# Sigmoid attention and a swish MLP on one core: the table of steps made anew

## The chip, the core and the metric

The kernel runs on one core of one Trainium2 chip. The metric is the device time of one execution in microseconds, the median of several runs. The engines are TensorE (PE: matmuls; PEld: its weight loads), VectorE (DVE), ScalarE (ACT), GpSimd (POOL) and SyncE (SP). Each works through its own queue in order, and they meet at semaphores.

## The reference, cut to what matters

```python
batch, n_heads, seq, head_dim = (8, 12, 448, 64)
n_tokens, d_model, d_ff = (3584, 768, 2048)

# attention, per batch and head
scores = scale * np.matmul(q, k.transpose(0, 1, 3, 2)) - np.log(S)
attn = 1.0 / (1.0 + np.exp(-scores))
attn_out = np.matmul(attn, v)
# heads side by side: one row of 768 for each of 8 * 448 tokens
x = attn_out.transpose(0, 2, 1, 3).reshape(B * S, H * D)
# the MLP
h = x @ w_in
g = h * (1.0 / (1.0 + np.exp(-beta * h)))
out = g @ w_out
```

Inputs and output are float32; the kernel computes in fp16 with sums in PSUM in float32.

## The kernel before, in words

The work is cut into 24 groups of four heads (three groups for each of the 8 batches), and the MLP into batches of 448 tokens and, for the second product, pairs of 128-token tiles. The first batch's MLP is a plain product (`dense1`, `dense2`). From the second batch on both products of the MLP go by a Strassen-Winograd scheme: seven half-size products P1 to P7 instead of eight, for which weights, tokens and hidden values have to be added up first, in fp16.

Nothing in the code decides the order of the work but a table written into it. `OPENING + STEPS` is a list of 842 short names; `follow` walks it and calls one function for each name, and each engine's queue gets its instructions in that order. The names that matter here:

- `V g.jt` (`visit`): the scores of group g for one block of 128 keys: 8 matmuls on TensorE (L239), then two sigmoids on ScalarE (L251). The last block (jt 3) has 64 keys, and there two groups are done together: 16 matmuls, which need the transposes of both.
- `R g.r` (`transpose`): VectorE transposes the queries (r 0, L217) or keys (r 1, L225 and L229) of group g. `Q g` loads them from GpSimd's queue (L133) into one of three buffers named in `RAW_HOMES`.
- `K b` (`load_v`): v of batch b, six DMAs from GpSimd's queue (L153 four times, L160 twice), into one of two buffers. `E b` (`double_v_last`): VectorE copies its last rows (L167). `A g` (`attend`): attention times v for group g, 16 matmuls (L321) and two casts to fp16 on VectorE (L335).
- `X b.i` (`token_sum`): fp16 sums of tokens on VectorE, xs or xT. `S`, `T` (`weight_sum`): fp16 sums of the weights, w_S and w_T, once for all batches. `H t.i` (`hidden_sum`): fp16 sums of hidden values, "sum".
- `I b.d.i` (`wino1`): product Pi of the MLP's first half for batch b and block d: six matmuls of 224 columns (L192), then a sum or sigmoid. P1 opens PSUM bank x and P2 fills it further, P7 opens z and P4 fills it further, after VectorE has added up what P7 left. A product that fills a bank further has to wait for that.
- `G b.d`, `B b.d.j` (`weigh_right`, `weigh_below`): two or one sigmoids on ScalarE, and a product into gt on GpSimd (L520 for G, L530 for B).
- `U t.i.part` (`wino2`): half of product Pi of the second half for tiles t and t + 1: four matmuls of 384 columns (L192). Finished tiles are stored from SP's queue.
- `D`, `f`, `O`: the plain products of the first batch; `l`, `k`, `w`, `o`: loads of q, k and weights in the opening; `h`, `y`, `z`, `r`: visits, attention and transposes of half a group in the opening.

All sums, fp16 or not, go through one helper, `add`, so they share the line L406; the tile names tell them apart: "osb" has an input in PSUM, "w_T", "w_S", "xs", "xT" and "sum" are fp16 in SBUF throughout. Dense matmuls have one helper too, L192. It splits each of them into two of 64 columns when the next attention or score step in the table is an `A` or `y`:

```python
tiled["cols"] = D if then in ("A", "y") else P
```

Output buffers, and the buffers for q and k, are taken from seven homes, in the order of `OUT_HOMES` and `RAW_HOMES`.

Of the kernel before, what the change touches and what calls it, by code (L numbers as in the profile page):

```python
# [13 lines left out]
def kernel(  # L14
# [390 lines left out]
    def add(out, in0, in1, op=ALU.add):  # L405
# [275 lines left out]
    def follow(steps):  # L681
# [30 lines left out]
        B2.2.0 R12.0 V11.2 I2.3.4 U6.1.0 H6.2 U6.1.1 B2.3.0 B2.3.1 V12.2 I3.0.1 U6.2.0 H6.0
        H6.1 U6.2.1 A11 G2.3 X3.0 V12.1 X3.2 U6.6.0 U6.5.0 X3.1 U6.6.1 U6.5.1 V12.3 I3.0.2
        Q15 H6.3 K5 I3.0.6 U6.3.0 I3.0.5 U6.3.1 X3.3 I3.0.7 V12.0 Q18 I3.0.3 G3.0 H8.0
        U6.7.0 I3.0.4 H8.1 B3.0.0 U6.7.1 A12 V13.1 U8.1.0 H8.2 R15.1 U6.4.0 U6.4.1 U8.5.0
        U8.6.0 R14.1 E5 R15.0 Q16 U8.1.1 V13.2 U8.6.1 H8.3 U8.5.1 I3.1.1 U8.2.0 V13.0 U8.3.0
        U8.2.1 I3.1.6 U8.3.1 U8.7.0 B3.0.1 I3.1.5 U8.7.1 I3.1.7 I3.1.2 R14.0 I3.1.3 U8.4.0
        I3.1.4 U8.4.1 V14.2 I3.2.1 G3.1 R16.0 I3.2.6 A13 V14.0 Q17 B3.1.0 I3.2.2 I3.2.5
        B3.1.1 I3.2.7 I3.3.1 I3.2.3 V14.1 I3.2.4 I3.3.6 B3.2.0 I3.3.5 G3.2 U10.1.0 R16.1
        I3.3.2 I3.3.7 B3.2.1 I3.3.3 V14.3 I3.3.4 B3.3.1 I4.0.1 H10.2 B3.3.0 X4.0 U10.1.1 A14  # L720
        H10.0 X4.1 V15.2 G3.3 U10.2.0 U10.2.1 H10.1 I4.0.2 U10.5.0 V16.1 U10.6.0 U10.6.1
        I4.0.6 U10.5.1 U10.7.0 H10.3 I4.0.5 H12.0 X4.3 X4.2 V15.1 U10.3.0 R17.1 U10.7.1
        U10.3.1 V15.0 H12.2 I4.0.3 U10.4.0 U10.4.1 R17.0 R18.0 U12.1.0 Q19 H12.1 K6 A15
# [140 lines left out]
```

## Time and profile before

| | |
|---|---|
| median of 3 runs | 369.17 us (369.03 to 369.20) |
| the profiled execution | 369.55 us |
| its span in the profile | 367.7 us |
| granted TensorE clock | 0.998 |
| TensorE busy | 360.5 us, 98% |
| VectorE, ScalarE, GpSimd busy | 277.7, 248.0, 157.3 us |

Times in the profile run from the start of the span. A row of the timeline has the start and the duration in us, engine, line, operation, what it writes and reads, shapes, and how many instructions it merges; in brackets stand the idle time of the engine before it and what ended that. Matmuls are pipelined, and their ends are modelled, so the distance from start to start is the safer measure of them.

### The profile page before, as it was taken

The numbers are of one execution on the slowest core, as the hardware profiler recorded it, in microseconds if no ns is written. First come the engines' busy times: TensorE is split into PE (matmuls) and PEld (weight loads), VectorE is DVE, ScalarE is ACT, GpSimd is POOL, SyncE is SP. The second block draws the span as 40 slices with busy tenths as digits, with TensorE's granted clock in tenths as the row PEclk, the third lists the DMA queues.
The fourth block names the chain that finished last, engine by engine and source line by source line (L and its number), as shares of the span: only waits on it lengthen the run. The fifth ranks groups of instructions, "written<-read, shape, count | busy, mean of one in ns | idle before, by whom it ended". The sixth has DMA issues, their size and how long they took to land.

```text
span 367.7 us, 9364 instructions
## 1 busy us (share of the span) xinstructions
PE 360.5 (98%) x3795; PEld 238.6 (65%) x3795; DVE 277.7 (76%) x524; ACT 248.0 (67%) x410; POOL 157.3 (43%) x192
## 2 busy tenths in 40 slices
PE   8999999999999999999999999999999999999996
PEld 3577754466456875657865777657856587788564
DVE  5346768989886697867869767797898477889574
ACT  5988976886766797654984778777976568436210
POOL 7734513117514376611762433922541227228400
PEclk9999999999999999999999999999999999999999
DMA  8999999909179111953309040686001230010225
GB/s 169 188 200 198 200 204 204 228 9 123 25 158 145 42 34 18 180 117 85 55 7 194 16 92 3 120 100 138 3 0 45 45 87 2 0 34 11 46 70 187
DMA packets 42699, 34.77 MB, mean 95 GB/s; under 512 B 21904, under 2 KB 39200, under 8 KB 42656
## 3 DMA queue, kind: packets, MB, share of 16 engines
q0 software_dynamic: 36688, 22.47, 44.3%
q1 hardware_dynamic: 5968, 11.71, 12.1%
q8 instruction: 29, 0.48, 0.5%
q14 instruction: 14, 0.11, 0.1%
HBM read 45.62 MB, written 11.01 MB: 154 GB/s over the span
## 4 chain that ended last, share of the span: by engine, by line
PE 85%; DMA 5%; DVE 4%; POOL 4%; issue 1%; ACT 1%; DVEq 0%; ACTq 0%; POOLq 0%
PE m_ps L192 67%; PE sco L239 10%; PE av_ps L321 8%; DMA raw<-in_q_dram 3%; POOL gt L530 2%; DMA raw<-in_k_dram 2%; DVE osb L406 2%; DVE sum L406 1%; POOL w_in L174 1%; ACT sg L459 1%; POOL raw L133 1%; DVE w_T L406 1%; DVE xs L406 0%; DVE xT L335 0%; DVE qT L217 0%
## 5 line engine op out<-in xcount | busy, mean ns | idle before, releaser
L251 ACT ACTIVATE attnT<-sco 128x896 f16<-128x896 f32 (+1 forms) x163 | 139.3, 908 | 59.1 <-PE sco L239 58.5
L406 DVE TENSOR_TENSOR osb<-m_ps,osb 128x448 f32<-128x448 f32 (+2 forms) x197 | 115.3, 595 | 47.8 <-PE m_ps L192 40.8
L192 PEld LDWEIGHTS <-w_in 128*128 128x128 f16 (+1 forms) x1014 | 81.1, 101 | 20.3 <-issue 12.9
L530 POOL TENSOR_TENSOR gt<-osb,sg 128x448 f16<-128x448 f32 x52 | 60.6, 1180 | 67.5 <-ACT sg L459 65.6
L192 PE MATMUL m_ps<-xT,w_in 128*128 128x224 f16 (+3 forms) x804 | 84.2, 267 | 0.0
L459 ACT ACTIVATE sg<-osb,beta_sb 128x448 f32<-128x448 f32 (+1 forms) x104 | 54.7, 578 | 9.3 <-DVE osb L406 9.1
L192 PEld LDWEIGHTS <-sum 128*128 128x128 f16 (+1 forms) x456 | 39.8, 100 | 27.3 <-issue 5.2
L520 POOL TENSOR_TENSOR gt<-osb,sg 128x448 f16<-128x448 f32 x26 | 30.4, 1172 | 58.3 <-ACT sg L459 55.5
L239 PE MATMUL sco<-qT,kT 32*128 32x448 f16 (+3 forms) x864 | 51.5, 340 | 1.4 <-DVE kT L229 0.5
L192 PEld LDWEIGHTS <-gt 128*128 128x128 f16 (+1 forms) x484 | 37.4, 103 | 23.7 <-issue 6.1
L192 PE MATMUL m_ps<-w_out,gt 128*128 128x384 f16 (+2 forms) x340 | 52.7, 323 | 0.0
L192 PEld LDWEIGHTS <-w_S 128*128 128x128 f16 (+1 forms) x516 | 44.1, 100 | 7.8 <-issue 4.9
L192 PE MATMUL m_ps<-w_out,sum 128*128 128x384 f16 (+1 forms) x232 | 41.1, 327 | 0.0
L192 PE MATMUL m_ps<-w_T,sum 128*128 128x384 f16 (+1 forms) x224 | 40.8, 327 | 0.0
L321 PE MATMUL av_ps<-attnT,v 128*64 128x448 f16 (+3 forms) x400 | 38.0, 343 | 0.0
L192 PE MATMUL m_ps<-xs,w_S 128*128 128x224 f16 (+1 forms) x342 | 36.5, 259 | 0.4 <-DVE xs L406 0.4
L335 DVE CAST xT<-av_ps 128x448 f16<-128x448 f32 (+1 forms) x54 | 28.2, 564 | 8.3 <-PE av_ps L321 8.2
L133 POOL DMA_DIRECT2D raw<-in_q_dram x26 | 15.0, 579 | 42.0 <-DVE qT L217 16.4
L321 PEld LDWEIGHTS <-v 128*64 128x64 f16 (+1 forms) x432 | 20.8, 108 | 17.2 <-issue 8.2
L459 ACT ACTIVATE osb<-m_ps,beta_sb 128x224 f32<-128x224 f32 x52 | 20.3, 451 | 12.5 <-PE m_ps L192 11.5
L239 PEld LDWEIGHTS <-kT 32*128 32x128 f16 (+1 forms) x864 | 13.3, 96 | 23.8 <-issue 19.9
L363 DVE TENSOR_TENSOR gt<-m_ps,sg 128x224 f16<-128x224 f32 (+1 forms) x40 | 16.3, 432 | 11.9 <-ACT sg L360 11.8
(53 smaller groups left out, 310.0 us busy)
## 6 DMA issues: line engine op xcount, KB each, us to landing
out_dram<-osb SPq DMA_DIRECT2D x100, 96.0 KB, 1.9
raw<-in_k_dram POOLq DMA_DIRECT2D x23, 224.0 KB, 5.4
raw<-in_q_dram POOLq DMA_DIRECT2D x21, 224.0 KB, 3.8
v<-in_v_dram POOLq DMA_DIRECT2D x32, 144.0 KB, 6.5
w_in<-in_moe_w_in_dram POOLq DMA_DIRECT2D x8, 384.0 KB, 10.7
w_out<-in_moe_w_out_dram POOLq DMA_DIRECT2D x4, 768.0 KB, 13.5
v<-in_v_dram POOLq DMA_DIRECT2D x16, 48.0 KB, 6.1
out_dram<-osb SPq DMA_DIRECT2D x4, 192.0 KB, 2.1
```

The costliest lines, as they stand in the source:

```text
L133: nc.gpsimd.dma_start(out=raws[g][:, r, c0:c1].rearrange("p c d -> p (c d)"), in_=(q, k)[r][b, HQ * t : HQ * (t + 1)].rearrange("h (p c) d ...
L174: nc.gpsimd.dma_start(out=w_in16[:, :, c * n : (c + 1) * n], in_=moe_w_in[:, c * n : (c + 1) * n].rearrange("(c p) f -> p c f", p=P),)
L192: nc.tensor.matmul(to[c : c + step], hidden[:, c : c + step], weights, **({} if step == P else {"tile_position": (0, c)}), **flags,)
L239: nc.tensor.matmul(sco[base : base + nk, hh, u0 : u0 + n], kT[g][lo : lo + BLK, jt * P : jt * P + nk, e], qT[g][lo : lo + BLK, c0 : c0 + n ...
L251: nc.scalar.activation(out=at[:, :, 0:n], in_=sco[:, :, 0:n], func=AF.Sigmoid, bias=NEG_LOG_S, scale=MSCALE,)
L321: nc.tensor.matmul(av[hh * D : (hh + 1) * D, 0:n], vs[b][base : base + nk, 2 * (s % NPAIR) + hh, jt], at[base : base + nk, hh, 0:n], start ...
L335: nc.vector.tensor_copy(out=xTs[b][:, s % NPAIR, c0 : c0 + n], in_=av[:, 0:n])
L363: nc.vector.tensor_tensor(out=gt[:, dc, off : off + n], in0=m1[:, 0:n], in1=sg[:, 0:n], op=ALU.mult)
L406: nc.vector.tensor_tensor(out=out, in0=in0, in1=in1, op=op)
L459: nc.scalar.activation(out=out, in_=in_, func=AF.Sigmoid, bias=0.0, scale=beta_sb[:, dc : dc + 1])
L520: nc.gpsimd.tensor_tensor(out=gt[:, 2 * d : 2 * d + 2, off : off + QH], in0=ob[:, 0], in1=sg, op=ALU.mult)
L530: nc.gpsimd.tensor_tensor(out=gt[:, dc, off : off + S].rearrange("p (h n) -> p h n", h=2), in0=oa[:, :, j], in1=sg, op=ALU.mult,)
```

## The change

The same set of steps is put in another order: `OPENING`, `STEPS`, `RAW_HOMES` and `OUT_HOMES` are made anew, and no other line differs. No function changes, and no step is added or dropped. The change says of itself that VectorE's fp16 sums and GpSimd's products are kept apart in it by when each is ready.

As nearly every line of the table differs, here are the stretches that the prediction speaks of, old and new, with the steps around them.

```diff
-    RAW_HOMES = "012012012012201202121021"
+    RAW_HOMES = "012012012012012020120120"
...
 # opening
-    h0.1.0 y1.0 Q3 z1.0 h0.1.1 r1.1 y2.0 w6 Q4 z2.0 h1.1.0 w7 f0 f3 p0 f1 f4 r2.1 h1.1.1
-    f2 K1 f5 o0.0 y0.1 Q5 z0.1 h2.1.0 f6 f7 o1.0 f9 f8 o0.1 h2.1.1
+    y1.0 z1.0 w5 h0.1.1 r1.1 Q3 y2.0 w6 z2.0 Q4 p0 w7 h1.1.0 f3 f1 f0 f4 K1 r2.1 h1.1.1
+    f2 f5 o0.0 y0.1 z0.1 h2.1.0 f6 Q5 f7 f8 f9 o1.0 o0.1 h2.1.1
...
 # from A6 to A9, old
-    O1.1.7 E2 D1.10 R8.0 D1.2 V6.3 T1.0 D1.11 R10.0 D1.0 X1.3 A6 V7.1 D1.9 T1.1 D1.1
-    I1.3.1 X1.2 I1.2.1 V7.0 R8.1 I1.3.6 I1.3.5 I1.3.2 I1.2.2 I1.3.7 I1.3.3 Q9 V7.2
-    I1.3.4 I1.2.6 K3 I1.2.5 T4.1 U2.1.0 I1.2.7 B1.3.0 I1.2.3 B1.3.1 V8.0 I1.2.4 B1.2.0
-    H2.2 U2.1.1 A7 B1.2.1 V8.1 U2.2.0 H2.0 H2.1 X2.0 T4.0 R9.0 U2.2.1 U2.7.0 G1.3 R9.1
-    V8.2 U2.5.0 U2.6.0 U2.6.1 U2.5.1 H2.3 G1.2 V8.3 U2.7.1 A8 V9.1 U2.4.0 R10.1 Q13 H4.0
-    U4.1.0 U2.3.0 R11.1 V9.2 H4.1 U2.3.1 U4.1.1 U4.6.0 Q12 X2.1 H4.2 V9.0 U2.4.1 U4.6.1
-    X2.2 R11.0 E3 I2.0.1 R13.1 U4.2.0 X2.3 A9 V10.3 U4.2.1 I2.0.2 I2.0.6 U4.5.0 H4.3
...
-    S3.0 U4.5.1 Q14 I2.0.5 V10.0 K4 U4.7.0 U4.3.0 U4.3.1 V10.1 I2.0.3 G2.0 I2.0.7 U4.7.1
 # from A6 to A9, new
+    D1.1 V6.0 T2.1 D1.8 D1.0 V6.3 Q10 O0.1.7 S4.0 I1.3.1 T2.0 K4 A6 R9.1 R10.0 V7.1
+    D1.10 D1.11 X1.2 V7.0 I1.3.6 I1.3.2 I1.3.5 I1.2.1 X1.3 I1.3.7 I1.3.3 V7.2 I1.3.4
+    B1.3.1 I1.2.6 I1.2.5 B1.3.0 I1.2.7 R8.0 I1.2.2 I1.2.3 I1.2.4 R9.0 H2.2 S3.0 G1.3
+    V8.0 U2.1.0 U2.1.1 Q11 B1.2.0 B1.2.1 A7 H2.0 V8.1 U2.7.0 U2.2.0 H2.1 R10.1 G1.2
+    U2.2.1 T4.0 X2.0 V8.2 U2.5.0 U2.6.0 U2.6.1 U2.5.1 H2.3 V8.3 H4.0 U2.7.1 A8 V9.1 H4.1
+    U2.3.0 Q12 U2.3.1 U4.5.0 X2.1 V9.2 T4.1 U4.1.0 U4.1.1 H4.2 U4.6.0 K3 U4.6.1 U4.2.0
+    R11.1 V9.0 U2.4.0 R12.0 H4.3 X2.3 R11.0 U2.4.1 R12.1 E3 Q16 U4.2.1 U4.7.0 U4.5.1 A9
...
 # behind the last visit, old
-    B6.3.0 V23.1 U20.2.0 H20.0 H20.1 G6.3 U20.2.1 A23 U20.7.0 X7.0 I7.0.1 X7.1 I7.1.1
-    U20.6.0 X7.2 U20.6.1 H20.3 I7.0.6 U20.5.0 X7.3 I7.0.5 I7.0.2 I7.1.6 I7.0.7 U20.5.1
 # behind the last visit, new
+    I6.1.2 I6.1.3 I6.3.1 I6.1.4 V23.1 U18.7.0 B6.1.0 I6.3.6 U18.7.1 G6.1 I6.3.5 I6.2.1
+    I6.2.6 U20.1.0 B6.0.1 I6.2.5 I6.2.2 I6.3.2 I6.2.7 I6.2.3 U18.4.0 I6.2.4 B6.1.1
+    I6.3.7 B6.2.0 I6.3.3 G6.3 I7.2.1 B6.2.1 A23 I6.3.4 I7.1.1 X7.0 X7.1 I7.0.1 U20.1.1
+    U18.4.1 B6.3.1 I7.2.6 B6.3.0 I7.0.6 G6.2 I7.0.5 I7.1.6 H20.0 H20.1 I7.1.5 I7.0.2
+    I7.0.3 I7.1.2 X7.2 I7.2.2 H20.2 U20.6.0 U20.2.0 I7.2.5 I7.0.7 I7.1.3 G7.0 U20.6.1
```

Both tables end with the same steps of tiles 26 and 27, U26.2.1 last.

More of the change, by code (lines that the diff above doesn't have):

```diff
@@ L712 @@
[L712 to L723, printed above, removed]
@@ new lines @@
+        U2.3.0 Q12 U2.3.1 U4.5.0 X2.1 V9.2 T4.1 U4.1.0 U4.1.1 H4.2 U4.6.0 K3 U4.6.1 U4.2.0
+        R11.1 V9.0 U2.4.0 R12.0 H4.3 X2.3 R11.0 U2.4.1 R12.1 E3 Q16 U4.2.1 U4.7.0 U4.5.1 A9
+        V10.0 X2.2 U4.3.0 E4 I2.0.1 U4.3.1 I2.0.6 U4.7.1 V10.3 Q13 I2.0.5 U4.4.0 I2.0.2
+        I2.0.3 G2.0 U4.4.1 I2.1.1 I2.1.6 I2.1.5 V10.1 Q14 I2.1.2 I2.1.7 I2.0.7 I2.1.3 G2.1
+        V10.2 I2.1.4 I2.0.4 I2.2.1 B2.0.0 B2.0.1 I2.2.6 A10 B2.1.1 V11.0 R13.0 I2.2.5 I2.2.2
+        I2.3.1 I2.2.7 B2.1.0 I2.2.3 V11.1 I2.2.4 I2.3.6 G2.2 I2.3.5 I2.3.2 I2.3.7 B2.2.0
@@ new lines @@
+        V11.2 I2.3.3 U6.1.0 H6.2 I2.3.4 U6.1.1 B2.2.1 X3.0 A11 B2.3.1 B2.3.0 V12.2 I3.0.1
+        R13.1 X3.1 U6.7.0 U6.2.0 H6.0 H6.1 G2.3 U6.2.1 V12.0 R14.0 I3.0.6 U6.6.0 U6.6.1
+        I3.0.5 X3.2 V12.1 U6.5.0 I3.0.2 H6.3 R16.1 U6.5.1 K5 U6.7.1 I3.0.3 U6.3.0 V12.3
+        U6.3.1 X3.3 U6.4.0 A12 Q15 G3.0 V13.1 U6.4.1 I3.1.1 H8.0 I3.0.7 I3.1.6 U8.1.0 H8.1
+        V13.0 I3.1.5 I3.1.2 R14.1 I3.0.4 I3.1.3 U8.1.1 U8.6.0 H8.2 Q17 V13.2 G3.1 I3.1.7
+        R16.0 U8.6.1 U8.2.0 U8.5.0 I3.1.4 H8.3 U8.5.1 Q19 B3.0.0 B3.0.1 U8.2.1 A13 V14.2
@@ new lines @@
+        U8.3.0 I3.2.1 B3.1.1 I3.2.6 U8.7.0 V14.0 U8.7.1 U8.3.1 B3.1.0 E5 R15.1 I3.2.5 I3.2.2
+        U8.4.0 I3.2.7 U8.4.1 I3.2.3 V14.1 I3.3.1 I3.2.4 R15.0 I3.3.6 B3.2.0 I3.3.5 B3.2.1
+        I3.3.7 G3.2 I3.3.2 V14.3 I3.3.3 I3.3.4 U10.1.0 X4.0 U10.1.1 A14 B3.3.0 R17.1 B3.3.1
+        H10.0 H10.1 V15.2 I4.0.1 H10.2 X4.1 U10.2.0 R17.0 U10.2.1 V16.1 U10.5.0 U10.6.0 X4.2
+        G3.3 X4.3 I4.0.6 U10.6.1 V15.0 H10.3 I4.0.5 I4.0.2 U10.5.1 I4.0.7 I4.0.3 V15.1 K6
+        H12.0 I4.0.4 G4.0 U10.3.0 U10.7.0 U10.3.1 A15 V16.0 I4.1.1 R19.1 I4.1.6 I4.1.5
@@ new lines @@
+        B4.0.1 U10.7.1 H12.2 Q18 Q23 V16.3 B4.0.0 H12.1 I4.1.2 I4.1.7 I4.1.3 U10.4.0 V16.2
+        U10.4.1 I4.1.4 A16 G4.1 V17.2 B4.1.1 I4.2.1 B4.1.0 U12.1.0 U12.1.1 U12.6.0 U12.6.1
+        R18.0 I4.2.2 I4.2.6 I4.2.5 V17.0 I4.2.7 I4.2.3 U12.2.0 U12.2.1 H12.3 R23.1 G4.2
+        U12.5.0 V17.1 U12.5.1 I4.2.4 R19.0 I4.3.1 I4.3.6 U12.7.0 R18.1 Q20 U12.3.0 U12.3.1
+        B4.2.1 U12.7.1 I4.3.5 I4.3.7 B4.2.0 I4.3.2 I4.3.3 V18.3 I4.3.4 B4.3.1 E6 G4.3 X5.0
+        B4.3.0 Q21 U14.1.0 U12.4.0 U14.1.1 U12.4.1 A17 X5.2 R23.0 V18.0 I5.0.1 U14.2.0 X5.1
@@ new lines @@
+        I6.2.6 U20.1.0 B6.0.1 I6.2.5 I6.2.2 I6.3.2 I6.2.7 I6.2.3 U18.4.0 I6.2.4 B6.1.1
+        I6.3.7 B6.2.0 I6.3.3 G6.3 I7.2.1 B6.2.1 A23 I6.3.4 I7.1.1 X7.0 X7.1 I7.0.1 U20.1.1
+        U18.4.1 B6.3.1 I7.2.6 B6.3.0 I7.0.6 G6.2 I7.0.5 I7.1.6 H20.0 H20.1 I7.1.5 I7.0.2
+        I7.0.3 I7.1.2 X7.2 I7.2.2 H20.2 U20.6.0 U20.2.0 I7.2.5 I7.0.7 I7.1.3 G7.0 U20.6.1
+        I7.2.3 U20.5.0 G7.1 U22.1.0 X7.3 U20.5.1 I7.3.1 I7.1.7 I7.0.4 I7.2.7 U20.7.0 H20.3
+        U20.2.1 H22.0 I7.1.4 I7.3.6 G7.2 U20.7.1 H22.1 B7.0.0 I7.3.5 I7.3.2 I7.2.4 U24.1.0
@@ new lines @@
+        B7.1.1 B7.2.1 I7.3.3 B7.0.1 I7.3.7 U22.6.0 U20.3.0 B7.1.0 U22.1.1 I7.3.4 G7.3
+        U22.6.1 H22.3 U24.1.1 U22.5.0 U22.2.0 U22.5.1 B7.3.1 U20.3.1 U22.2.1 H22.2 H24.2
+        U22.3.0 U22.3.1 B7.3.0 U22.7.0 U24.2.0 B7.2.0 H24.0 U20.4.0 U26.1.0 U22.7.1 U24.2.1
+        U24.5.0 H24.1 U24.7.0 U24.6.0 U20.4.1 U24.6.1 U24.5.1 H26.0 H24.3 U26.1.1 U24.7.1
+        U22.4.0 H26.2 U22.4.1 U24.3.0 U24.3.1 U26.5.0 U24.4.0 U26.7.0 H26.1 U26.6.0 U26.6.1
+        U26.5.1 H26.3 U26.2.0 U26.7.1 U24.4.1 U26.3.0 U26.4.0 U26.3.1 U26.4.1 U26.2.1
```

65 lines of the change are left out of this document (22 added, 43 removed).

## The prediction

> **What bounds the kernel now.** I read the page first, then the chain that ended last, then the busy time by stretches, and last the timeline at the places where the stretches show TensorE idle.
>
> ```profile
> PE 360.5 (98%) x3795; PEld 238.6 (65%) x3795; DVE 277.7 (76%) x524; ACT 248.0 (67%) x410; POOL 157.3 (43%) x192
> ...
> 25.00:84.00 59.00, 59.00 (x639) 36.79 (x632) 46.25 (x96) 47.81 (x78) 20.42 (x34) 1.00 1.11 174
> 84.00:99.00 15.00, 13.67 (x142) 8.32 (x141) 13.84 (x22) 11.11 (x18) 10.01 (x12) 1.00 0.55 65
> 99.00:313.00 214.00, 213.92 (x2318) 144.16 (x2316) 165.80 (x303) 153.65 (x252) 93.74 (x106) 1.00 0.43 73
> 313.00:319.00 6.00, 5.61 (x49) 3.65 (x46) 5.21 (x9) 2.49 (x6) 1.89 (x2) 1.00 0.00 0
> 319.00:364.40 45.40, 45.37 (x349) 33.38 (x347) 35.21 (x61) 13.43 (x29) 14.69 (x12) 1.00 0.23 64
> ```
>
> TensorE is busy for 98% of the span, no other engine for more than 76%. The stretches (duration, then busy time of each engine) say where the other 2% lie: 25 to 84 us has 59.00 of 59.00 busy, 99 to 313 has 213.92 of 214.00, the last 45.40 have 45.37. Only 84 to 99 (13.67 of 15.00) and 313 to 319 (5.61 of 6.00) hold waits. So a new order of the same work can gain only what TensorE waits, and can lose wherever it makes TensorE wait anew.
>
> ```profile
> 13.40 10.70 DMA raw<-in_q_dram
> 24.59 0.58 PE sco L239 x16
> ...
> 100.86 0.51 PE sco L239 x8
> 101.36 2.06 PE m_ps L192 x12
> ...
> 110.58 0.53 PE sco L239 x16
> ```
>
> This is the chain in order of time (start, duration). The end of the first 25 us is set by a load of q that lands at 24.1, after which TensorE starts its scores at 24.59 and the chain stays on TensorE but for the two stretches named. The rows also give its pace: eight score matmuls take 0.51 us up to the next group, sixteen 0.53, and twelve matmuls of 384 columns with the change to scores behind them 2.06.
>
> Matmul ends are modelled, so I take the waits from start to start. First place:
>
> ```profile
> 86.01 2.96 POOL L530 TENSOR_TENSOR gt<-osb,sg 128x448 f16<-128x448 f32 x2
> 86.18 1.80 DVE L406 TENSOR_TENSOR w_T<-w_out,w_T 128x1536 f16<-128x1536 f16 x1
> 87.18 0.57 PE L239 MATMUL sco<-qT,kT 32*128 32x448 f16 x8
> 87.90 1.14 DVE L406 TENSOR_TENSOR osb<-m_ps,osb 128x448 f32<-128x448 f32 x2
> 88.56 0.77 PE L192 MATMUL m_ps<-xs,w_in 128*64 128x224 f16 x12 [0.81 <-DVE osb L406]
> 89.13 0.84 PE L192 MATMUL m_ps<-w_out,gt 128*64 128x384 f16 x8
> 89.78 1.64 PE L321 MATMUL av_ps<-attnT,v 128*64 128x448 f16 x16
> ```
>
> From the eight scores at 87.18 (step V8.0) to the next matmuls at 88.56 (I1.2.4) pass 1.38 us instead of 0.51: 0.87 lost. The row says what ended it: a VectorE sum into osb. That one (the sum of I1.2.7, whose bank I1.2.4 fills further) stood in VectorE's queue behind the weight sum w_T (T4.1) of 1.80 us, which ran beside GpSimd's products for B1.3. Second place:
>
> ```profile
> 94.89 1.15 POOL L520 TENSOR_TENSOR gt<-osb,sg 128x448 f16<-128x448 f32 x1 [1.72 <-ACT sg L459]
> 94.96 1.90 DVE L406 TENSOR_TENSOR w_T<-w_out,w_T 128x1536 f16<-128x1536 f16 x1
> 96.78 0.63 DVE L217 STREAM_TRANSPOSE qT<-raw 128x448 f32<-128x448 f32 x1
> 97.13 0.39 PE L239 MATMUL sco<-qT,kT 32*64 32x448 f16 x4
> 97.80 0.20 DVE L229 STREAM_TRANSPOSE kT<-raw 128x64 f32<-128x64 f32 x1
> 98.05 0.59 PE L239 MATMUL sco<-qT,kT 32*64 32x448 f16 x12 [0.53 <-DVE kT L229]
> 98.57 0.84 PE L192 MATMUL m_ps<-w_T,sum 128*64 128x384 f16 x8
> 98.94 0.57 POOL L133 DMA_DIRECT2D raw<-in_k_dram  x1
> 99.02 0.68 DVE L406 TENSOR_TENSOR sum<-gt,sum 128x1024 f16<-128x1024 f16 x1
> ```
>
> Step V8.3 scores group 8 and group 9 together: sixteen matmuls, from 97.13 to 98.57, 1.44 us instead of 0.53: 0.91 lost. It waits for the transposes of group 9 (R9.0, R9.1) at 96.78 to 98.00, which stand behind the other weight sum T4.0 (1.90 us), again beside a product (G1.3). Third place:
>
> ```profile
> 314.20 1.20 POOL L520 TENSOR_TENSOR gt<-osb,sg 128x448 f16<-128x448 f32 x1 [0.51 <-ACT sg L459]
> 314.44 1.51 DVE L406 TENSOR_TENSOR sum<-sum,gt 128x1024 f16<-128x1024 f16 x1
> 316.17 1.46 PE L192 MATMUL m_ps<-w_T,sum 128*128 128x384 f16 x8
> 317.46 0.51 DVE L406 TENSOR_TENSOR xs<-xT,xs 128x672 f16<-128x672 f16 x1
> 318.03 0.75 PE L192 MATMUL m_ps<-xs,w_S 128*128 128x224 f16 x6 [0.39 <-DVE xs L406]
> ...
> L406 DVE TENSOR_TENSOR w_T<-w_out 128x1536 f16<-128x1536 f16 x2 | 1.9, 954 | 0.1
> L406 DVE TENSOR_TENSOR sum<-gt,sum 128x1024 f16<-128x1024 f16 x13 | 8.8, 680 | 0.0
> ```
>
> Four whole matmuls of 384 columns take 0.65 us (89.13 to 89.78, there as eight halves), so the eight at 316.17 should hand over at 317.47; the next start at 318.03: 0.56 lost. I7.0.6 waits for the token sum X7.1 at 317.46, late because the hidden sum H20.1 took 1.51 us beside the product G6.3.
>
> The last two rows (mean duration at the end) give the price of the meetings: such a weight sum takes 0.954 us and such a hidden sum 0.680 when no product runs beside it. So 1.80, 1.90 and 1.51 are 0.85, 0.95 and 0.83 too long, and the waits that follow, 0.87, 0.91 and 0.56, are about that. 314.20 + 1.20 + 0.55 is the end of the sum: it seems to do most of its work after the product ends. VectorE's sums with an input from PSUM keep their length beside products (2 in 1.14 at 87.90).
>
> One smaller wait has another cause:
>
> ```profile
> 133.51 1.31 PE L192 MATMUL m_ps<-xs,w_S 128*128 128x224 f16 x12
> 134.66 1.31 PE L192 MATMUL m_ps<-xT,w_in 128*128 128x224 f16 x12
> 136.06 0.73 PE L192 MATMUL m_ps<-xT,w_S 128*128 128x224 f16 x6
> ```
>
> Twelve matmuls of 224 columns take 1.15 us (133.51 to 134.66), the next twelve 1.40: 0.25 lost, to a run of four plain sums on VectorE.
>
> **The change part by part.** *Work.* Every engine has the same operations as before, but for TensorE: 3,843 matmuls for 3,795, since 48 dense ones more stand just ahead of an attention step and are split into two halves of 64 columns. A pair of halves costs what a whole one does (the eight halves at 89.13 end after 0.65 us), so this costs nothing, with no cover needed. Score, attention and dense matmuls change over as often as before (77 times out of scores and 55 times from dense ones into them, in both programs). So TensorE's own work stays.
>
> *Opening.* GpSimd issues its loads in the same order up to the third batch's v, and the load of q that ends at 24.1 stands where it stood, with the same matmuls ahead of it. f3 now stands ahead of f0 and so needs the second part of w_in one step sooner; whatever it waits is hidden as long as it ends before the 24.59 at which q lets TensorE go on. Cost 0; without that cover, one step of six matmuls, 0.6.
>
> *First place.* Steps I1.2.5 to I1.2.4 now have neither T4.0 nor T4.1 among them; both weight sums stand after A7, near V8.2 and V9.2. Between I1.2.5 and I1.2.4 VectorE has only its sums, one product into gt and one transpose (R8.0, 0.63 by the row at 96.78). Gain 0.87; what is late next is VectorE's sum for I1.2.7, covered by I1.2.2 and I1.2.3 on TensorE (1.15 us by the row at 133.51).
>
> *Second place.* R9.1 now stands after A6, R9.0 ahead of V8.0: three visits of scores earlier. Gain 0.91. T4.0 now stands two steps behind G1.2, so it can still meet that product and take 1.90; behind it wait X2.0 and the evictions of U2.1 to U2.6, for which V8.2, U2.5 and U2.6 give TensorE over 2.5 us of work. T4.1 is read first by U2.4.1, six half steps and a visit later (6 x 0.65 + 0.5 = 4.4 us). Bounds: 0 to 0.95 lost again, I take 0.
>
> *Third place.* H20.0 and H20.1 now come after X7.0 and X7.1. From A23 to I7.2.6, the first user of X7.1, TensorE has three steps of six matmuls (0.58 each) and two half steps (0.65): 3.0 us. VectorE has in that time two casts (0.55 each), one sum (0.6) and X7.0, X7.1 (0.5 each): 2.7 us. The margin of 0.3 is thin, and a product that meets X7.0 or X7.1 takes it. Gain 0.16 to 0.56; I take 0.36.
>
> *The wait that is added.* v of batch 4 (K4) is now loaded ahead of v of batch 3 (K3), and takes the buffer that batch 1 left. K3 has to wait for batch 2's: its first DMA waits on GpSimd's queue until A8 has ended, and A9 needs it. Behind it on that queue stand the loads Q16 and Q13 and the products of batch 2; the loads are for visits much later, and the first product is not ready before A9 is through.
>
> ```profile
> L153 POOL DMA_DIRECT2D v<-in_v_dram x32: 609/639/726, 3.5 to 237.3; - x32
> L167 DVE COPY v<-v x8: 354/354/665, 13.3 to 258.7; 64x768 f16<-64x768 f16 x8
> ...
> DMA to landing us min/median/max: 4.9/6.4/10.9
> ```
>
> TensorE has thirteen half steps and three visits between A8 and A9: 13 x 0.65 + 3 x 0.5 + 0.1 = 10.1 us. GpSimd needs some 0.3 to begin, three further issues of 0.64 and a landing of 6.4 for the rows that A9 starts with: 8.6 us. The last rows and their copy E3 (0.35) come at 0.3 + 5 x 0.64 + 6.4 + 0.4 = 10.3, and are read when twelve of A9's sixteen matmuls are done (12/16 of 1.64, so at 11.3). That is 1.0 us of cover: cost 0 at the median landing. With the slowest landing of the row, 10.9, it is 4.5 us later, and 3.5 us are lost. I take 0, since 6.4 is the middle of 48 such loads and 10.9 the one slowest.
>
> While K3 is issued and lands, VectorE's queue holds six sums of fp16 (T4.1, two token sums, three hidden sums: 0.95 + 2 x 0.5 + 3 x 0.68 = 4.0 us). The issue at 98.94 ran under the sum of 99.02 and took 0.57 us, and the slowest of 32 issues of v took 0.73: this trace shows no sum that holds an issue up. The Trainium skill (SBUF — State Buffer, section "SBUF: two separate sides", the box on the "DVE blocks DMA" trap) speaks against the change here: a DMA from GpSimd's queue can't have its descriptors written while VectorE runs an operation in a mode that holds their shared port. By that rule the sum would have up to 3 us more in it, as an estimate.
>
> *Homes and other loads.* Loads and output buffers change place; stores stay behind their steps. TensorE waited for none of them after 25 us in the rows above. Cost 0, 0 to 0.3 kept for the range.
>
> The sum, on the profiled execution of 369.55 (span 367.7): 0.87 + 0.91 + 0.36 = 2.14 less. The median, 369.17, stands 0.38 below that execution, and the same difference from it gives 369.17 - 2.14 = 367.0. The 0.25 at 136 stays in the sum.
>
> **The rivals.** *A, meetings elsewhere.* Nothing but the order keeps sums and products apart, and T4.0 still follows G1.2. In the old order three meetings cost TensorE time; were two of the new one to cost 0.9 each, the gain would be 2.14 - 1.8 = 0.3: 368.8. For it: VectorE is the next busiest engine, and the margin at the third place is 0.3. Against it: both weight sums have left the places where a step waits right behind them.
>
> *B, the late v.* K3 lands late, A9 waits, and all that follows. It decides from a landing of 7.4 us on; each further us is lost whole, and from 9.5 on the kernel is slower than before. At the slowest row: 369.17 - 2.14 + 3.5 = 370.5. For it: a landing of 10.9 has happened. Against it: the median is 6.4.
>
> *B2, sums hold the load up.* If K3's six DMAs could not proceed while the six sums run, it would come 4.0 us later, 3.0 beyond its cover: 370.0. The issue at 98.94 under a sum speaks against it. This is the rule of the Trainium skill's box above, as a mechanism of this kernel.
>
> *C, no effect.* The waits were slack: another limit close behind TensorE takes the time again, 369.2. Against it: after 99 us TensorE is busy 213.92 of 214.00, so what it starts earlier it ends earlier.
>
> **How the numbers follow.** A measurement of this kernel tells some 0.2% (0.74 us) from no change. Forecast 0.76, at 367.0; its own range runs from 366.3 (all of the third place and the 0.25 gained too, 366.6, and 0.3 for homes) to 367.9 (one wait of 0.9 comes back). A 0.10 at 368.8, of which 0.04 lie beyond 0.2% faster. C 0.04. B 0.06, of which 0.04 are slower by over 0.2%, the rest below. B2 0.04. So faster 0.76 + 0.04 + 0.01 = 0.81, same 0.06 + 0.04 + 0.01 = 0.11, slower 0.08. The range from 366.1 to 369.1 leaves out 0.10 above and some 0.05 below.
>
> **What would show it.** Right: no gap over 0.3 us ahead of I1.2.4, ahead of V8.3 and behind A23; the weight sums w_T below 1.4 us or without a waiting TensorE behind them; the span from 84 us on shorter by some 2 us, with next to no TensorE idle in any stretch; GpSimd's first K3 issue waiting for the attention of A8, and A9 not waiting for v. Wrong: an idle time of TensorE ended by v or by E3 (B), by sums longer than 1 us at other places (A), or a TensorE that is busy for as long as before though the waits have gone (C).

## The result, and the profile after

The changed kernel takes 366.8 us (median), against 369.74 us for the kernel before in the same measurement: ratio 0.9923 (of the means), with an interval of 0.9902 to 0.9944. The time forecast was 367.0, in a range from 366.1 to 369.1. The first profiled execution of the changed kernel took 719.84 us with TensorE at half its pace from end to end, so it is left out of the ratio, and the profile shown here is of a further one, of 366.55 us with a span of 364.8.

Its page, TensorE's busy time and the chain that ended last, and then the busy time by stretches (TensorE first, then weight loads, VectorE, ScalarE, GpSimd; the granted clock third from the end):

```profile
PE 360.2 (99%) x3843; PEld 238.7 (65%) x3843; DVE 273.8 (75%) x524; ACT 247.0 (68%) x410; POOL 156.3 (43%) x192
...
PE 98%; ACT 0%; DVE 0%; issue 0%
...
25.00:84.00 59.00, 59.00 (x633) 36.80 (x632) 46.53 (x97) 47.84 (x77) 21.04 (x34) 1.00 1.20 184
84.00:99.00 15.00, 15.00 (x159) 8.68 (x161) 14.01 (x26) 12.22 (x20) 9.46 (x10) 1.00 0.38 62
99.00:313.00 214.00, 214.00 (x2379) 145.86 (x2372) 164.55 (x301) 154.19 (x255) 92.57 (x104) 1.00 0.41 70
313.00:319.00 6.00, 6.00 (x60) 5.48 (x58) 5.84 (x11) 3.13 (x9) 2.26 (x3) 1.00 0.30 68
319.00:361.00 42.00, 42.00 (x304) 29.07 (x302) 30.75 (x56) 10.15 (x21) 14.24 (x12) 1.00 0.26 64
```

TensorE's own busy time is what it was (360.2 for 360.5). From 25 us on it is busy in every stretch for the whole of it: the 1.33 us of idle time between 84 and 99 and the 0.39 between 313 and 319 are gone, and so are the 0.08 between 99 and 313. Measured between the starts of matmuls, from the first scores behind the load of q to the last matmul of all, 339.53 us (24.59 to 364.13) have become 336.84 (24.37 to 361.21): 2.69 less. The first scores start 0.22 earlier: q landed earlier in this execution, and TensorE did not have to wait for it. Over the runs below they start at 24.21 to 24.65 in the new table and at 24.57 to 24.86 in the old one, so a part of the 0.22 may belong to the new opening; no run separates it. Together that is 2.91, beside 2.88 less span (367.65 to 364.78) and 3.00 less time (369.55 to 366.55).

The timeline at the three places, in the new order. First and second place:

```profile
85.63 0.74 PE L192 MATMUL m_ps<-xT,w_S 128*128 128x224 f16 x6
86.30 0.73 PE L192 MATMUL m_ps<-xs,w_in 128*128 128x224 f16 x6
86.97 0.58 PE L239 MATMUL sco<-qT,kT 32*128 32x448 f16 x8
93.49 1.40 POOL L520 TENSOR_TENSOR gt<-osb,sg 128x448 f16<-128x448 f32 x1 [1.05 <-ACT sg L459]
94.44 1.27 DVE L406 TENSOR_TENSOR w_T<-w_out,w_T 128x1536 f16<-128x1536 f16 x1
96.12 0.60 PE L239 MATMUL sco<-qT,kT 32*64 32x448 f16 x16
96.65 0.84 PE L192 MATMUL m_ps<-w_T,sum 128*64 128x384 f16 x8
101.85 0.95 DVE L406 TENSOR_TENSOR w_T<-w_out,w_T 128x1536 f16<-128x1536 f16 x1
```

I1.2.4 (86.30) is followed by the next scores after 0.67 us, and V8.3 (96.12) scores its two groups in 0.53, with no wait. Ahead of I1.2.4 a small one is left: the step before it, six matmuls of 224 columns, takes 0.67 (85.63 to 86.30) where six take 0.575, so 0.09 of the 0.87 stayed. The weight sum T4.1 takes 0.95 at 101.85. T4.0, at 94.44, did meet the product G1.2 of 93.49 and took 1.27, but nothing on TensorE waits for it: the meeting that the prediction allowed for came, and it cost nothing. Third place:

```profile
310.47 0.64 DVE L406 TENSOR_TENSOR xs<-xT 128x672 f16<-128x672 f16 x1
311.14 0.51 DVE L406 TENSOR_TENSOR xs<-xT,xs 128x672 f16<-128x672 f16 x1
311.80 3.04 PE L192 MATMUL m_ps<-xs,w_S 128*128 128x224 f16 x30
315.84 0.69 DVE L406 TENSOR_TENSOR sum<-sum,gt 128x1024 f16<-128x1024 f16 x1
```

X7.0 (310.47) met the end of a product and took 0.64 instead of some 0.50. X7.1 behind it ends at 311.65 (311.14 + 0.51), 0.15 us before the first matmul that uses it, and H20.1 takes 0.69 at 315.84, behind the products.

### The profile page after: what moved, and what is told of

It reads as the page before. It is cut to its first block, busy times and chain, and to the rows that moved or that the text cites. A ratio compares the mean times of both kernels' runs of the same rounds, so it can differ in the third digit from the quotient of the medians.

```text
span 718.1 us, 9451 instructions
## 1 busy us (share of the span) xinstructions
PE 713.7 (99%) x3843; PEld 357.3 (50%) x3843; DVE 282.7 (39%) x524; ACT 254.8 (35%) x410; POOL 155.4 (22%) x192
## 4 chain that ended last, share of the span: by engine, by line
PE 99%; DVE 0%; issue 0%
PE m_ps L192 78%; PE sco L239 10%; PE av_ps L321 10%; PE idle_ps L795 2%; DVE osb L406 0%; DVE gt L788 0%
## 5 line engine op out<-in xcount | busy, mean ns | idle before, releaser
L192 PE MATMUL m_ps<-xT,w_in 128*128 128x224 f16 (+2 forms) x798 | 166.4, 429 | 0.0
L192 PEld LDWEIGHTS <-w_in 128*128 128x128 f16 (+1 forms) x1014 | 124.4, 150 | 76.2 <-issue 40.4
L192 PE MATMUL m_ps<-w_out,gt 128*128 128x384 f16 (+2 forms) x350 | 103.9, 551 | 0.0
L192 PEld LDWEIGHTS <-w_S 128*128 128x128 f16 (+1 forms) x534 | 71.0, 157 | 34.1 <-issue 16.1
L192 PE MATMUL m_ps<-w_T,sum 128*128 128x384 f16 (+1 forms) x236 | 81.0, 560 | 0.0
L192 PE MATMUL m_ps<-w_out,sum 128*128 128x384 f16 (+1 forms) x248 | 80.4, 554 | 0.0
L321 PE MATMUL av_ps<-attnT,v 128*64 128x448 f16 (+3 forms) x400 | 71.6, 550 | 0.0
L192 PE MATMUL m_ps<-xs,w_S 128*128 128x224 f16 (+1 forms) x348 | 70.4, 421 | 0.0
L192 PE MATMUL m_ps<-w_T,gt 128*128 128x384 f16 (+1 forms) x136 | 41.3, 558 | 0.0
L192 PE MATMUL m_ps<-xT,w_S 128*128 128x224 f16 (+1 forms) x186 | 37.3, 421 | 0.0
```

The source lines that it names most:

```text
L192: nc.tensor.matmul(to[c : c + step], hidden[:, c : c + step], weights, **({} if step == P else {"tile_position": (0, c)}), **flags,)
L321: nc.tensor.matmul(av[hh * D : (hh + 1) * D, 0:n], vs[b][base : base + nk, 2 * (s % NPAIR) + hh, jt], at[base : base + nk, hh, 0:n], start ...
```

## The experiments

Every ratio is against the kernel before, measured on the same chip at the same time (median 369.65 for the twelve small loads and for the three moves together; 369.66 for T4.1 back, the four small loads and the two runs on splitting; 369.49 for the others). Start-to-start numbers go from the first scores behind the load of q to the last matmul, as above, so that the landing of that load, which varied between executions (first scores at 24.21 to 24.86), is kept out.

**The changed kernel once more.** No edit.

> The changed kernel once more, for a trace that can be laid beside that of before. Both theories: 0.992 of the time before. Theory (the three waits are gone): no gap of TensorE over 0.3 us from start to start at I1.2.4, V8.3 and behind A23, and 2.1 to 2.9 us less in all. Rival (the gain is elsewhere, in the opening or in TensorE's own pace): the first scores after the load of q start earlier than 24.5, or the same groups of matmuls take fewer us.

Measured: 366.55 us, ratio 0.9920 (0.9903 to 0.9937). It is the execution that is read above.

**One part alone: the two weight sums of the first and second place, moved in the old table.**

```diff
 # the kernel before
-    I1.3.4 I1.2.6 K3 I1.2.5 T4.1 U2.1.0 I1.2.7 ...
+    I1.3.4 I1.2.6 K3 I1.2.5 U2.1.0 I1.2.7 ...
-    H2.2 U2.1.1 A7 B1.2.1 V8.1 U2.2.0 H2.0 H2.1 X2.0 T4.0 R9.0 ...
+    H2.2 U2.1.1 A7 B1.2.1 V8.1 U2.2.0 H2.0 H2.1 X2.0 R9.0 ...
-    ... H2.3 G1.2 V8.3 U2.7.1 A8 ...  U4.1.0 U2.3.0 R11.1 V9.2 H4.1 U2.3.1
+    ... H2.3 G1.2 V8.3 T4.0 U2.7.1 A8 ...  U4.1.0 U2.3.0 R11.1 V9.2 H4.1 T4.1 U2.3.1
```

> The table of before with two steps moved: T4.0 from ahead of R9.0 to behind V8.3, T4.1 from behind I1.2.5 to behind H4.1. Theory (the weight sums stand ahead of what a step waits for): the first two waits, 0.87 and 0.91, go, the third stays: 1.8 us less, about 0.9952 of before. Rival (TensorE is held by something else there, and the gain of the new table comes from its many other differences): within 0.3 us of before.

Measured: 367.96 us, ratio 0.9957 (0.9942 to 0.9973). By stretches and in the timeline:

```profile
84.00:99.00 15.00, 15.00 (x162) 8.92 (x160) 12.83 (x23) 12.52 (x19) 10.15 (x12) 1.00 0.57 66
...
98.25 0.95 DVE L406 TENSOR_TENSOR w_T<-w_out,w_T 128x1536 f16<-128x1536 f16 x1
103.03 0.94 DVE L406 TENSOR_TENSOR w_T<-w_out,w_T 128x1536 f16<-128x1536 f16 x1
```

Both weight sums are down to 0.95, the stretch from 84 to 99 has no idle time left, and the third place keeps its wait (5.61 busy of 6.00 from 313 to 319). Two steps moved by a few places, with the rest of the old order kept, are 1.75 of the 2.69 us (339.53 to 337.79).

**One part alone: the product of the third place, moved in the old table.**

```diff
 # the kernel before
-    B6.3.0 V23.1 U20.2.0 H20.0 H20.1 G6.3 U20.2.1 A23 ...
+    B6.3.0 V23.1 U20.2.0 H20.0 H20.1 U20.2.1 A23 ...
-    U20.6.0 X7.2 U20.6.1 H20.3 I7.0.6 ...
+    U20.6.0 X7.2 U20.6.1 G6.3 H20.3 I7.0.6 ...
```

> The table of before with one step moved: G6.3 from between H20.1 and U20.2.1 to behind U20.6.1, so that its product no longer runs beside the hidden sum H20.1, which itself stays in its place. Theory (the product lengthens the sum): H20.1 takes 0.68 instead of 1.51 us, and the wait ahead of I7.0.6 of 0.56 goes or falls below 0.1: 0.5 us less, about 0.9986. Rival (the sum is late by its place in VectorE's queue, whatever GpSimd does): no change, the wait stays over 0.4.

Measured: 369.06 us, ratio 0.9992 (0.9978 to 1.0006), which by itself decides nothing: the effect is smaller than the interval. The trace decides:

```profile
313.00:319.00 6.00, 6.00 (x54) 4.17 (x51) 5.11 (x9) 2.51 (x6) 1.83 (x2) 1.00 0.00 0
...
314.45 0.69 DVE L406 TENSOR_TENSOR sum<-sum,gt 128x1024 f16<-128x1024 f16 x1
318.16 1.34 DVE L406 TENSOR_TENSOR sum<-gt,sum 128x1024 f16<-128x1024 f16 x1
```

H20.1 takes 0.69, the wait of 0.56 is gone, and the last matmul starts 0.56 earlier (363.57 for 364.13). The profiled execution as a whole took 371.09 us, because 5.75 us lie behind the start of its last matmul instead of 3.53; the cause of that is not known, and it is another reason to compare from start to start. The moved product, at 317.81, met another hidden sum instead, at 318.16, which then took 1.34, and no matmul waited. The meeting as such costs nothing; the wait behind it does.

**The suspected cause taken away: no product beside the sums.** Four of GpSimd's 78 products, those of B1.3.0, B1.3.1, G1.3 and G6.3, are left out of the kernel before (gt gets the sigmoid alone there). The order stays the old one.

```diff
 # the kernel before, in weigh_right; likewise in weigh_below for (1, 3)
+        if (b, d) in ((1, 3), (6, 3)):
+            for j in range(2):
+                sigmoid(gt[:, 2 * d + j, off : off + QH], ob[:, 0, j], 2 * d + j)
+            return
         nc.gpsimd.tensor_tensor(
 ...
```

> The table of before, no step moved. For B1.3.0, B1.3.1, G1.3 and G6.3 the product on GpSimd is left out: ScalarE writes the sigmoid alone into gt, so four of 78 blocks of g lack the factor h. Theory (the meeting of product and sum costs the time): both weight sums take 0.95 and H20.1 0.68 us, and of the three waits at most 0.3 us are left: 2.0 to 2.4 us less, about 0.994. Rival (the order of VectorE's queue alone costs it): the sums are shorter at most by a little, and less than 0.7 us are gained.

Measured: 367.27 us, ratio 0.9946 (0.9927 to 0.9966).

```profile
84.00:99.00 15.00, 15.00 (x159) 8.96 (x157) 13.36 (x24) 12.21 (x19) 6.37 (x9) 1.00 0.57 65
313.00:319.00 6.00, 6.00 (x56) 5.16 (x54) 5.49 (x12) 1.85 (x4) 0.00 (x0) 1.00 0.00 0
...
86.15 0.95 DVE L406 TENSOR_TENSOR w_T<-w_out,w_T 128x1536 f16<-128x1536 f16 x1
94.14 0.95 DVE L406 TENSOR_TENSOR w_T<-w_out,w_T 128x1536 f16<-128x1536 f16 x1
312.54 0.69 DVE L406 TENSOR_TENSOR sum<-sum,gt 128x1024 f16<-128x1024 f16 x1
```

With each step where it was and only the products gone, the sums take 0.95, 0.95 and 0.69 instead of 1.80, 1.90 and 1.51, and all three waits go (0.03 us are left at I1.2.4): 2.37 us from start to start (339.53 to 337.16). This is the run that shows the cause, since no step moved.

**One part undone: T4.1 back beside the products of B1.3, in the new table.**

```diff
 # the changed kernel
-    B1.3.1 I1.2.6 I1.2.5 B1.3.0 I1.2.7 R8.0 ...
+    B1.3.1 I1.2.6 I1.2.5 B1.3.0 T4.1 I1.2.7 R8.0 ...
-    U2.3.0 Q12 U2.3.1 U4.5.0 X2.1 V9.2 T4.1 U4.1.0 ...
+    U2.3.0 Q12 U2.3.1 U4.5.0 X2.1 V9.2 U4.1.0 ...
```

> The changed table with one step moved back: T4.1 from behind V9.2 to behind B1.3.0, ahead of I1.2.7, where the old table has it. Theory (a weight sum that meets a product costs TensorE what stands behind it): the sum takes 1.4 to 1.9 us again, TensorE waits 0.7 to 1.7 us at I1.2.4, and the kernel is that much slower than the changed one, about 0.995 to 0.996 of before. Rival (its place is harmless in the new order, since I1.2.2 and I1.2.3 cover it): no wait over 0.3 us, 0.992 as the changed one.

Measured: 368.34 us, ratio 0.9962 (0.9947 to 0.9976).

```profile
84.00:99.00 15.00, 13.62 (x142) 8.14 (x141) 14.15 (x24) 11.29 (x20) 10.19 (x10) 1.00 0.27 39
...
85.48 2.95 POOL L530 TENSOR_TENSOR gt<-osb,sg 128x448 f16<-128x448 f32 x2 [12.70 <-ACT sg L459]
85.71 1.73 DVE L406 TENSOR_TENSOR w_T<-w_out,w_T 128x1536 f16<-128x1536 f16 x1
85.91 0.74 PE L192 MATMUL m_ps<-xT,w_S 128*128 128x224 f16 x6
88.03 0.73 PE L192 MATMUL m_ps<-xs,w_in 128*128 128x224 f16 x6 [1.38 <-DVE osb L406]
```

The meeting and the wait are back: 1.73 us for the sum, and I1.2.4 starts 2.12 us after the step before it, where the changed kernel has 0.67 there (85.63 to 86.30). From start to start 338.29, so 1.45 more than the changed kernel: all of it this one wait.

**The added wait, with its cover taken.** Four small loads (HQ is 4) to a spare tile stand behind the first of K3's six loads.

```diff
 # the changed kernel, in load_v
+            for x in range(HQ if (b, i) == (3, 0) else 0):
+                queue.dma_start(
+                    out=spare[x * BLK : (x + 1) * BLK],
+                    in_=rows[:, 0, x * D : (x + 1) * D],
+                )
```

> The changed kernel with four small loads (32 x 64, to a spare tile that nothing reads) put behind the first of K3's six DMAs, so that the rest of v for A9 comes later. The ring of eight DMA semaphores then also makes the fifth of K3's loads wait for the landing of the first: its last rows and their copy come some 13.3 us after A8 instead of 10 to 10.3. Theory (A9's cover is 1.0 us from the rows): 1.5 to 2.2 us lost ahead of A9's last four matmuls, with TensorE idle until E3 or a load of v, about 0.997 of before. Rival (the cover is over 3 us): 0.992 as the changed one.

Measured: 367.14 us, ratio 0.9929 (0.9912 to 0.9947). The expectation of a loss of 1.5 us or more was wrong. First the changed kernel at this place, with the landing times of K3's loads in the last row; then the run with the four loads:

```profile
98.87 0.57 PE L239 MATMUL sco<-qT,kT 32*128 32x448 f16 x8
101.73 1.22 POOL L160 DMA_DIRECT2D v<-in_v_dram  x2
109.08 1.61 PE L321 MATMUL av_ps<-attnT,v 128*64 128x448 f16 x16
109.36 0.38 DVE L167 COPY v<-v 64x768 f16<-64x768 f16 x1
...
DMA to landing us min/median/max: 3.4/5.8/6.9
```

```profile
103.69 1.25 POOL L165 DMA_DIRECT2D v<-in_v_dram  x2
109.86 0.35 DVE L172 COPY v<-v 64x768 f16<-64x768 f16 x1 [0.61 <-DMA v<-in_v_dram]
...
DMA to landing us min/median/max: 3.4/5.3/5.6
```

The last two loads of K3 are issued 1.96 us later (103.69 for 101.73), but the slowest landing is 5.6 us for 6.9. So the last rows come at about 109.86, some 0.6 later than in the changed kernel (102.34, the last issue, plus 6.9 is 109.24). Their copy E3 ends at 110.21, and A9 wants it at 110.30, so next to nothing is lost. The duration of a landing was not a constant to be added to the issue; why it became shorter was not tried. The expectation also counted on the fifth of K3's loads waiting until the first had landed. The first, issued at 99.28, landed after 3.4 us, at 102.65, ahead of the fifth's issue at 103.69, so that wait cost nothing.

**The same with twelve small loads.** They are narrower, 16 columns each.

```diff
 # the changed kernel, in load_v
+            for x in range(3 * HQ if (b, i) == (3, 0) else 0):
+                queue.dma_start(
+                    out=spare[x % HQ * BLK : (x % HQ + 1) * BLK, x // HQ * 16 : x // HQ * 16 + 16],
+                    in_=rows[:, 0, x * 16 : x * 16 + 16],
+                )
```

> The changed kernel with twelve small loads to a spare tile behind the first load of K3, so K3's other five are issued some 12 x 0.49 = 5.9 us later (four small ones took 1.96 before). With four small loads the last of K3 landed at 109.86, and its copy E3 ended at 110.21, just as A9 wanted it (110.3): the cover was used up. Theory (K3's cover is some 2 us, and what comes later is lost whole): four further microseconds of delay make A9 start or end 4 us later, so the time is 3 to 4.5 us above the changed kernel's, ratio to the kernel before 1.000 to 1.006, with the wait of TensorE at 109 to 113 ended by v. Rival (the landing shortens as the issue comes later, as it did by more than 1 us with four, so a late v hardly costs anything): less than 1.5 us lost, ratio below 0.997.

Measured: 371.63 us, ratio 1.0056 (1.0040 to 1.0072): slower than the kernel before, as the rival of the late v had it. In the stretches below, the granted clock is the number behind GpSimd's.

```profile
107.60 1.29 POOL L165 DMA_DIRECT2D v<-in_v_dram  x2
112.42 2.97 PE L326 MATMUL av_ps<-attnT,v 128*64 128x448 f16 x16 [3.09 <-DMA v<-in_v_dram]
113.12 0.35 DVE L172 COPY v<-v 64x768 f16<-64x768 f16 x1 [3.80 <-DMA v<-in_v_dram]
115.31 0.66 PE L244 MATMUL sco<-qT,kT 32*128 32x448 f16 x8
...
112.00:113.00 1.00, 0.58 (x4) 0.42 (x6) 0.00 (x0) 0.00 (x0) 0.00 (x0) 0.57 1.15 197
113.00:115.00 2.00, 2.00 (x14) 0.75 (x10) 0.91 (x2) 0.00 (x0) 0.00 (x0) 0.50 1.10 237
115.00:116.00 1.00, 1.00 (x13) 0.23 (x10) 0.58 (x2) 0.00 (x0) 0.00 (x0) 0.72 1.11 215
```

A9 starts at 112.42 after a wait for v. From start to start the kernel has 341.53, so 4.69 more than the changed one. The wait itself is 3.25 of that (the last matmuls ahead of it start at 109.00, and the next would have come 0.17 later). The rest follows the wait: TensorE's clock stands at half until about 115.6, and A9 takes 2.89 us up to the next scores (112.42 to 115.31) instead of 1.54 (109.08 to 110.62).

**All dense matmuls split, and none.** The change splits 48 more of them than the order before; these two runs go to the ends.

```diff
 # the changed kernel: all split / none split
-            tiled["cols"] = D if then in ("A", "y") else P
+            tiled["cols"] = D
-            tiled["cols"] = D if then in ("A", "y") else P
+            tiled["cols"] = P
```

> The changed kernel with every dense matmul split into two of 64 columns, some 1,700 pairs in place of 386. Theory (a pair costs what a whole one does): TensorE's steps keep their length, 0.575 for six of 224 columns and 0.65 for four of 384, and the kernel is within 1 us of the changed one (0.990 to 0.995 of before). Rival (a pair costs 0.01 to 0.03 us more, through its second weight load): 10 us and more slower, over 1.02.

> The changed kernel with no dense matmul split. Theory (what a split saves is the change of shape ahead of an attention step): 0.1 us more at each of 24 attention steps behind dense ones, 2 to 2.5 us slower than the changed kernel, 0.998 to 0.999 of before. Rival (the split is worth nothing): 0.992 as the changed one.

Measured: all split, 368.09 us, ratio 0.9968 (0.9949 to 0.9987); none split, 369.19 us, ratio 0.9996 (0.9979 to 1.0013). The timeline from the dense steps ahead of A7 to the scores behind it, first of the changed kernel, then of the run with none split:

```profile
87.47 1.49 PE L192 MATMUL m_ps<-w_out,gt 128*64 128x384 f16 x16
88.80 1.61 PE L321 MATMUL av_ps<-attnT,v 128*64 128x448 f16 x16
90.35 0.57 PE L239 MATMUL sco<-qT,kT 32*128 32x448 f16 x8
```

```profile
88.21 1.47 PE L192 MATMUL m_ps<-w_out,gt 128*128 128x384 f16 x8
89.62 1.64 PE L321 MATMUL av_ps<-attnT,v 128*64 128x448 f16 x16
91.19 0.57 PE L239 MATMUL sco<-qT,kT 32*128 32x448 f16 x8
```

All split: 1,746 further pairs of halves make the work 0.85 us longer from start to start (337.69 for 336.84), half a nanosecond for each. The median is 1.5 above that of the changed kernel; the profiled execution is 1.15 above, and 0.47 us of that lies behind the start of the last matmul (4.03 us to the end of the span for 3.56), whose cause was not tried. None split: the eight dense matmuls take 1.41 up to the attention instead of 1.33, and the attention 1.57 instead of 1.55, so 0.10 at this place. There are 22 such places, and the work is 2.35 longer (339.19). The split is worth that much, but both tables have 22 of them, so it is no part of the change's gain.

**The three moves together in the old table.** The two edits in the old table shown above, the one of T4.0 and T4.1 and the one of G6.3, at once.

```diff
 # the kernel before, beside the moves of T4.0 and T4.1 shown above
-    B6.3.0 V23.1 U20.2.0 H20.0 H20.1 G6.3 U20.2.1 A23 ...
+    B6.3.0 V23.1 U20.2.0 H20.0 H20.1 U20.2.1 A23 ...
-    U20.6.0 X7.2 U20.6.1 H20.3 I7.0.6 ...
+    U20.6.0 X7.2 U20.6.1 G6.3 H20.3 I7.0.6 ...
```

> The kernel before with only the three moves of the earlier runs made together: T4.0 from ahead of R9.0 to behind V8.3, T4.1 from behind I1.2.5 to behind H4.1, G6.3 from ahead of U20.2.1 to behind U20.6.1; all else as before. Theory (the gain of the change is the waits behind sums that meet products, and the rest of the new order is worth nothing): 0.87 + 0.91 + 0.56 = 2.34 less from the first scores after the load of q to the last matmul (339.53 before, so 337.2), ratio 0.9935 to 0.9945. Rival (the waits come back elsewhere when all three moves are made, or the new order as a whole is needed): 338 or more, ratio above 0.996.

Measured: 367.37 us, ratio 0.9937 (0.9924 to 0.9949).

```profile
84.00:99.00 15.00, 15.00 (x162) 9.06 (x158) 12.84 (x23) 12.52 (x19) 10.23 (x12) 1.00 0.58 70
99.00:313.00 214.00, 213.92 (x2318) 144.03 (x2314) 166.58 (x304) 153.08 (x252) 93.99 (x106) 1.00 0.44 73
313.00:319.00 6.00, 6.00 (x55) 4.92 (x52) 5.84 (x11) 2.01 (x5) 1.13 (x1) 1.00 0.00 0
...
37.34 1.90 PE L192 MATMUL m_ps<-xT,w_in 128*128 128x224 f16 x18 [0.40 <-DMA w_in<-in_moe_w_in_dram]
```

All three waits are gone at once; the 0.08 between 99 and 313 stay. From start to start it is 337.67, so 1.86 less, in an execution in which a load of w_in held TensorE up for 0.56 at 37.34; without that it is 2.42 less, and 2.34 was expected. Three names moved in a table of 842 bring nine tenths of the 2.69 that the new table brings from start to start. By the medians it is less, 2.28 (369.65 to 367.37) where the changed kernel has 2.94 (369.49 to 366.55); how many executions that load held up, the one trace doesn't tell.

## Why the prediction was right, point by point

The mechanism held. That the time came within 0.2 us, 366.8 for 367.0, is in part luck: 367.0 was counted from 369.17, the median of the first three executions, while in the same measurement as the changed kernel the kernel before took 369.74. The gain was 2.94 by these medians, where 2.14 had been forecast, and the points below say which terms were too small.

*What bounds the kernel.* It held that a new order can gain only what TensorE waits. Busy time of TensorE stayed (360.2 for 360.5), and of the 2.88 us of span 2.69 went between the first scores behind q and the last matmul, nearly all of it waits, as the sum below shows.

*First and second place, 0.87 and 0.91.* Both went whole with the two moves alone: 1.75 beside 1.78. In the new order 0.09 stayed at I1.2.4: the cover that the prediction named there, I1.2.2 and I1.2.3, fell that much short of the sum of I1.2.7, which ends at 86.25. That the cause is the product beside the weight sum, as the prediction read from the durations, is shown from both sides: products out, the waits go; T4.1 put back, 1.45 are lost.

*Third place, taken as 0.36 between 0.16 and 0.56.* This term was too small: the whole 0.56 came. The margin behind A23, put at 0.3 us, is 0.15 in the trace (X7.1 ends at 311.65, its matmuls start at 311.80): a product did meet X7.0, as the prediction feared, but only with its end, and took 0.14 of the margin. H20.1 is no longer ahead of X7.0 and X7.1 in VectorE's queue.

*The small wait of 0.25 at 136, left in the sum.* It went too in the new order, and so did one of 0.15 ahead of 221.64 that the prediction did not name (six matmuls took 0.72 there instead of 0.575). In the changed kernel the 0.09 at I1.2.4 is the longest lateness of a matmul after 24.5 us. The waits that went sum to 0.87 + 0.91 + 0.56 + 0.25 + 0.15 - 0.09 = 2.65, beside 2.69 measured. The forecast of 2.14 was short by the 0.20 of the third place and by these 0.40. Neither of the two small waits was tried alone. The one ahead of 221.64 ends just behind a plain VectorE sum into osb (until 221.59), and no product runs at that time, so it is no meeting.

*T4.0 beside G1.2, 0 to 0.95, taken as 0.* The meeting came (1.27 us), and the cover named, the work of V8.2, U2.5 and U2.6, held.

*48 more split matmuls, 0.* Right: at 0.5 ns a pair, as the run with all split has it, they cost some 0.02 us.

*The added wait, 0 with 1.0 us of cover.* The cost was right, and the times of the estimate came out well: 10.2 us from A8 to A9 (98.87 to 109.08) for 10.1, and the copy of the last rows ended 10.9 after A8 (109.74) for 10.3. So 0.6 us were left ahead of 110.30, not 1.0. The price behind it, that each microsecond beyond the cover is lost whole, was too low where it was tried: with issues 5.9 us later the wait of 3.25 cost 4.69, of which 1.4 came after the wait, while the clock stood at half. The prediction had no term for that. And it counts from the landing, not from the issue: issues 2.0 us later cost next to nothing, because the landing became 1.3 shorter. The rival of the late v was a real danger with its size in the right order (371.6 measured for a kernel with the delay, 370.5 in the prediction for the slowest landing), and it did not come in the change.

*Sums that hold the load up.* The issues of K3 at 101.73 ran under the weight sum of 101.85 and took 1.22 for two, 0.61 each, where the middle of such issues in the trace before is 0.64; the slowest of K3's landings was 6.9. The Trainium skill (SBUF — State Buffer, section "SBUF: two separate sides", the box on the "DVE blocks DMA" trap) speaks of VectorE operations in a two-port mode and names a float32 copy as one. The prediction stretched the box to these fp16 sums of two inputs, which it does not name, and no hold-up showed in them.

*Meetings elsewhere, and no effect.* Meetings did stay in the new order (w_T 1.27 at 94.44; a hidden sum of 1.24 us at 336.23), with no matmul late behind them, so both rivals fell: 213.92 of 214.00 had been the right row to hold against the second.

## What to carry to other kernels

Where one engine is busy for nearly the whole of the span, look for the few stretches in which it is not, and ask what ended each wait: here five waits were all that an order could give between the load of q and the last matmul, and three moved names give nine tenths of it. A sum that meets another engine's work on a shared resource costs time only if something waits right behind it, so it is enough to move it (or its partner) to where nothing does. And before a load is put behind a wait, find its cover from issue, landing and first use, and do not carry the landing over as a constant.

## What the runs showed of the hardware

*Who comes second waits for the first.* In the run with T4.1 put back, the first product runs from 85.48 to 86.62 (1.14 of the 2.95 us), and the sum ends at 87.44, 0.82 later; the second product ends at 88.43, 0.99 behind the sum. A sum of 0.95 and a product of 1.14 thus each need their own length, less some 0.14, once the other has ended. T4.0 at 94.44 fits: the product ends at 94.89, the sum 0.82 later. The Trainium skill (SBUF — State Buffer, section "SBUF: two separate sides") says that VectorE, with two inputs from SBUF, and a GpSimd operation that reads SBUF lock each other out for a whole instruction, whichever started first. The traces agree but for the 0.14.

*A pause of TensorE can cost its clock.* The waits of 0.9 us in the kernel before, and of 1.5 in the run with T4.1 put back, left the granted clock at 1.00. With the wait of 3.25 us ahead of 112.42 it fell to half, by the stretches shown from 112.14 to 115.56 (0.86, 2.00 and 0.56 us of them), which cost a further 1.4 us. The Trainium skill (TensorE: Matmul & The Clock Gate, section "Part 1: The HAM clock gate") has the gate close after an idle window of some 3.4 us and open after as long a busy one. With one such pause to go by, the trace agrees on the opening, after 3.4 us; the closing came sooner than that, some 2.8 us after TensorE's last matmul had ended (109.33 by the modelled ends).

*Going from whole to half-width tiles costs TensorE about 0.1 us.* With 22 dense blocks run whole (128 columns) ahead of an attention step (64 columns) the work took 2.35 us longer than with them as halves, some 0.1 for each, and the halves cost next to nothing (0.5 ns a pair). The Trainium skill (TensorEngine Tiling (Array Packing), section "Key Properties") says that a change of the tiling mode drains TensorE. The traces agree that this change costs time, and give its price here.
